# WO(0)'s layernorm in a fused two-layer transformer kernel: four DMA transposes in place of two and two on TensorE, with VectorE held to that layernorm

## The chip, the cores and the metric

One core of one Trainium2 chip runs the whole kernel. The metric is the device time of one execution in microseconds (us). Executions of one kernel agree here within about 0.2% (1238.64 to 1240.82 for the kernel before), so differences of a microsecond in 1240 need several runs and a trace. The "granted clock" is the share of its full clock that TensorE was allowed to run at, as the profile records it.

## The reference, cut to what matters

```python
x = A_x                                        # [1, 2048, 1024], bf16
x = x + attention(layernorm(x), wqkv, wo)      # local, dilated: 8 keys, stride 2, 32 heads of 32
x = x + ffn(layernorm(x), w1, b1, w2, b2)      # gelu, 3584 hidden
x = x + attention(layernorm(x), wqkv, wo)      # the same weights again
x = x + ffn(layernorm(x), w1, b1, w2, b2)
```

The kernel cuts the 2048 positions into four groups of 512. Group n of layer 1 is n = 0..3, of layer 2 n = 4..7. For each n there are the stages QKV(n), attention on VectorE, WO(n) (output projection, residual, layernorm), FFN1(n) and FFN2(n). TensorE needs the normalised tile transposed (features on partitions) to go on.

## The kernel before

All engines are programmed through a framework that orders each engine's instructions itself. The kernel can pin the order of its matmuls (each depends on the one before), and `hold()` on VectorE: no VectorE instruction written after it goes ahead of the last one written before it.

```python
def acc_tile():                                # six PSUM accumulators of 128x512 f32
    return psum.tile([P, T], F32, name="acc", bufs=6)

def ln_tile(t, tt, xnT, on_pe=False, ahead=False):
    mv, rstd = (...) if ahead else ln_stats(t)   # VectorE stats, POOL for 1/sqrt
    xn = ln_norm(t, mv, rstd)                    # VectorE; three buffers named xn
    if on_pe:
        late.append((xn, xnT[:, tt, :, :]))      # transposed later, by TensorE
        return
    sp.dma_start_transpose(xnT[:, tt, :, :], xn[:].rearrange("s (k p) -> s k p", p=P))

def gen_wo(n, pe_from=NTT):
    # ... cut: two weight loads
    for tt in range(NTT):                        # four tiles of 128 positions
        for dh in range(2):                      # a "chunk": 8 matmuls into one accumulator
            # ... cut: the matmuls
            vec.tensor_tensor(out=xs, in0=ps[:], in1=xs, op=ALU.add)
            yield
        ln_tile(t, tt, xnT, tt >= pe_from)

# the schedule around WO(0)
stage(q2, 18)                                    # QKV(2) up to two of eight V chunks
stage(gen_wo(0, 2))                              # tiles 2 and 3 kept for TensorE
stage(q2, sides=each(new_prod, 1, 0, 1, 4, 8) + at(4, transpose_late))   # the other six V chunks
stage(gen_ffn1(0), sides=at(4, attend, 1) + ...) # head sums of group 1 after five FFN1 chunks
# ...
stage(gen_ffn2(0), sides=... + at(23, hold) + at(23, ln_a, 3, None, True))
# then WO(1), QKV(3), ...
```

`new_prod` is VectorE's product of q and k for one slice of the heads, with sums into a tree; `attend` begins with the head sums on TensorE (accumulator `L`), which need the last sum of that tree. FFN2's results leave their accumulators through VectorE (`tmp<-acc`); this is called an eviction below. `x15` is the sixteenth and last tile of 128 positions, `ln_a(3)` the layernorm ahead of QKV(3), and SP the engine whose queue issues the weight loads and the DMA transposes.

## Time and profile before

| | before |
|---|---|
| time, median of the six runs of the comparison | 1239.13 us (1238.64 to 1240.82) |
| span of the profiled run | 1237.2 us |
| TensorE busy | 1231.2 us |
| longest wait of TensorE after the first 100 us | 1.02 us |

The page of the kernel before: busy time by engine, TensorE's granted clock in 40 slices, and the chain of work that ended last.

```profile
span 1237.2 us, 14039 instructions
...
PE 1231.2 (100%) x5841; PEld 632.9 (51%) x5841; DVE 840.0 (68%) x868; ACT 306.3 (25%) x477; POOL 94.3 (8%) x214
...
PEclk9999999999999999999999999999999999999999
...
PE 97%; DVE 1%; POOL 1%; DMA 0%; issue 0%; ACT 0%
```

TensorE (PE) is the bound. A busy PE only says that matmuls were in the pipe, but here 704 of them in a row take 152.05 us in the chain, 216 ns each, so there is hardly a gap. The list of who waited for whom, PE alone, from 100 us to the end:

```profile
PE acc L211 <- DVE xn L93: 1.0, 1, 1.0
```

One wait in 1137 us. Its surroundings in the timeline of the kernel before (columns: start, duration of the merged row, engine, operation, tiles, count, and in brackets the idle time ahead and what ended it):

```profile
139.24 8.80 PE L118 MATMUL acc<-xnT,wt 128*128 128x512 bf16 x40
...
143.57 2.28 DVE L93 TENSOR_TENSOR big<-big 128x4096 bf16<-128x4096 bf16 x1
...
145.89 2.29 DVE L93 TENSOR_TENSOR big<-big 128x4096 bf16<-128x4096 bf16 x1
146.05 2.18 POOL L93 TENSOR_TENSOR rstd<-mv,eps_t 128x1 f32<-128x1 f32 x1 [4.17 <-DVE mv L93]
...
147.87 0.61 PE L211 MATMUL acc<-ident,xn 128*128 128x128 bf16 x8
...
148.89 0.55 DVE L93 TENSOR_SCALAR xn<-x,mv,rstd 128x1024 bf16<-128x1024 bf16 x1 [0.71 <-POOL rstd L93]
...
149.50 0.62 PE L211 MATMUL acc<-ident,xn 128*128 128x128 bf16 x8 [1.02 <-DVE xn L93]
...
149.96 10.53 PE L118 MATMUL acc<-xnT,wt 128*128 128x512 bf16 x48
```

From 147.87 to 149.96 TensorE does 16 transposes and waits for the last tile, 2.09 us in all. The tile is late since VectorE put two sums of 2.2 us ahead of finishing its layernorm, and since POOL's add of one column, 0.2 us elsewhere, took 2.18 us beside the second of them.

### The profile page before, as it was taken

Reading aid. Unit: us, or ns where it says so; the run is one execution under the profiler, and the core shown is the slowest. Engines: PE = TensorE matmul, PEld = TensorE weight load, DVE = VectorE, ACT = ScalarE, POOL = GpSimd, SP = SyncE. Lnnn points to the kernel's source line nnn. Section 1 sums busy time; section 2 is a strip of 40 time slices with the busy share of each in tenths; the row PEclk is TensorE's granted clock in tenths of the full one; section 3 lists DMA queues with packets and bytes.
Section 4 is the critical chain, followed back from the end, with each engine's and each line's share of the span. In section 5 each row is a group of like instructions: output and inputs, shape, how many; then the busy total and the mean of one; then the engine's idle time right before and its main releaser. Section 6 shows DMA issues by size and latency. Waiting matters only on the chain.

```text
span 1237.2 us, 14039 instructions
## 1 busy us (share of the span) xinstructions
PE 1231.2 (100%) x5841; PEld 632.9 (51%) x5841; DVE 840.0 (68%) x868; ACT 306.3 (25%) x477; POOL 94.3 (8%) x214
## 2 busy tenths in 40 slices
PE   9999999999999999999999999999999999999998
PEld 6666544456444564445644455444654444444444
DVE  7989899996985899337994379843597788012001
ACT  4333252023420144101341023510235001300310
POOL 4010210012000100001000010100001002000000
PEclk9999999999999999999999999999999999999999
DMA  9954564576646555656556565566654568556441
GB/s 308 279 179 146 165 198 161 168 176 216 191 156 201 161 177 161 196 168 183 170 157 198 172 182 160 164 198 199 171 170 135 184 200 193 169 157 195 152 136 53
DMA packets 215327, 219.81 MB, mean 178 GB/s; under 512 B 66066, under 2 KB 184992, under 8 KB 212192
## 3 DMA queue, kind: packets, MB, share of 16 engines
q1 hardware_dynamic: 212592, 208.16, 54.7%
q0 software_dynamic: 2672, 10.76, 2.8%
q8 instruction: 45, 0.74, 0.2%
q14 instruction: 18, 0.15, 0.0%
HBM read 197.40 MB, written 6.29 MB: 165 GB/s over the span
## 4 chain that ended last, share of the span: by engine, by line
PE 97%; DVE 1%; POOL 1%; DMA 0%; issue 0%; ACT 0%
PE acc L118 97%; POOL rstd L93 1%; DVE stats L93 1%; PE L L118 0%; DVE x L93 0%; DMA x<-in_A_x_dram 0%; DVE xn L93 0%; DVE big L93 0%; PE acc L211 0%; DVE mv L93 0%; PE L L211 0%; ACT xnT L93 0%
## 5 line engine op out<-in xcount | busy, mean ns | idle before, releaser
L118 PE MATMUL acc<-xnT,wt 128*128 128x512 bf16 (+1 forms) x3376 | 721.7, 376 | 0.6 <-ACT xnT L93 0.6
L118 PEld LDWEIGHTS <-wt 128*128 128x128 bf16 x3376 | 398.6, 119 | 320.9 <-issue 3.9
L118 PE MATMUL acc<-wt,hT 128*128 128x512 bf16 (+1 forms) x1820 | 388.1, 376 | 0.0
L118 PEld LDWEIGHTS <-hT 128*128 128x128 bf16 x1820 | 178.1, 98 | 209.0
L93 DVE TENSOR_TENSOR big<-big 128x1024 bf16<-128x1024 bf16 (+2 forms) x184 | 244.2, 1359 | 1.8
L93 ACT ACTIVATE hT<-acc,b1T 128x512 bf16<-128x512 f32 x224 | 151.8, 687 | 319.8 <-PE acc L118 319.2
L93 DVE TENSOR_TENSOR big<-abc,vT 128x4096 bf16<-128x4096 bf16 x64 | 144.0, 2283 | 49.3 <-DMA abc<-a_d 49.3
L93 DVE TENSOR_TENSOR tmp<-acc,b2bc 128x512 f32<-128x512 f32 x56 | 38.6, 690 | 180.9 <-PE acc L118 177.4
L93 DVE TENSOR_TENSOR big<-qT,kT 128x4096 bf16<-128x4096 bf16 x64 | 143.8, 2285 | 23.7 <-ACT kT L93 23.1
L93 ACT CAST qT<-acc 128x512 bf16<-128x512 f32 x64 | 37.4, 586 | 329.2 <-PE acc L118 329.2
L118 PE MATMUL acc<-wt,oT 128*128 128x512 bf16 x448 | 97.9, 379 | 0.0
L93 DVE BATCH_NORM_STATS2 stats<-x 128x6 f32<-128x512 bf16 x128 | 83.7, 679 | 3.3 <-DMA x<-in_A_x_dram 2.7
L118 PEld LDWEIGHTS <-oT 128*128 128x128 bf16 x448 | 43.8, 98 | 52.9 <-issue 0.2
L93 DVE TENSOR_TENSOR x<-acc,big 128x512 bf16<-128x512 f32 (+1 forms) x9 | 5.7, 633 | 90.0 <-PE acc L118 90.0
L93 ACT CAST vT<-acc 128x512 bf16<-128x512 f32 x64 | 37.5, 586 | 83.7 <-PE acc L118 83.7
L93 POOL TENSOR_TENSOR rstd<-mv,eps_t 128x1 f32<-128x1 f32 x60 | 18.5, 308 | 502.3 <-DVE mv L93 502.3
L93 ACT CAST kT<-acc 128x512 bf16<-128x512 f32 x64 | 37.5, 586 | 71.7 <-PE acc L118 71.7
L93 POOL DMA_DIRECT2D a_d<-a x32 | 19.0, 620 | 410.7 <-DVE a L93 410.7
L93 DVE TENSOR_SCALAR xn<-x,mv,rstd 128x1024 bf16<-128x1024 bf16 x52 | 28.6, 550 | 30.0 <-POOL rstd L93 29.5
L93 DVE TENSOR_TENSOR x<-acc,x 128x512 bf16<-128x512 f32 x64 | 43.0, 672 | 6.1 <-PE acc L118 5.8
L93 DVE TENSOR_TENSOR x<-tmp,x 128x512 bf16<-128x512 f32 x56 | 38.6, 690 | 1.5
L93 POOL TENSOR_TENSOR rstd<-rstd,mhalf 128x1 f32<-128x1 f32 x60 | 33.9, 565 | 4.7
(54 smaller groups left out, 211.3 us busy)
## 6 DMA issues: line engine op xcount, KB each, us to landing
wt<-in_B_w_dram SPq DMA_DIRECT2D x56, 1024.0 KB, 5.5
wt<-in_B_w_dram SPq DMA_DIRECT2D x64, 896.0 KB, 4.7
wt<-in_A_wqkv_dram SPq DMA_DIRECT2D x46, 1024.0 KB, 5.6
wt<-in_A_wo_dram SPq DMA_DIRECT2D x16, 1024.0 KB, 4.9
abc<-a_d POOLq DMA_DIRECT2D x32, 256.0 KB, 4.6
x<-in_A_x_dram SPq DMA_DIRECT2D x16, 256.0 KB, 5.4
out_dram<-x SPq DMA_DIRECT2D x31, 128.0 KB, 1.8
wt<-in_A_wqkv_dram SPq DMA_DIRECT2D x4, 512.0 KB, 6.8
```

Source lines behind the costliest of these rows:

```text
L93: inst = f(*args, **kwargs)
L118: return pe(nc.tensor.matmul(*args, **kwargs))
```

## The change

Its intent: take the 16 transposes and their wait off TensorE. All four tiles of WO(0) go through DMA transposes; VectorE is held so that the products stand behind the layernorm; and the second W1 load is ordered behind the transposes on the SP queue, so that it does not delay them.

```diff
-    def ln_tile(t, tt, xnT, on_pe=False, ahead=False):
+    last_transpose = [None]
+
+    def ln_tile(t, tt, xnT, ahead=False):
         ...
-        if on_pe:
-            late.append((xn, xnT[:, tt, :, :]))
-            return
-        sp.dma_start_transpose(...)
+        last_transpose[0] = sp.dma_start_transpose(...)
@@ gen_ffn1
-            sp.dma_start(wt[:], w1_v[:, :, j4 * 4 * P:(j4 + 1) * 4 * P])
+            load = sp.dma_start(wt[:], w1_v[:, :, j4 * 4 * P:(j4 + 1) * 4 * P])
+            if n == 0 and j4 == 1:
+                dep_order(load, last_transpose[0], "transposes first")
@@ the schedule
-        stage(gen_wo(0, 2))
-        stage(q2, sides=each(new_prod, 1, 0, 1, 4, 8) + at(4, transpose_late))
+        new_prod(1, 4)
+        hold()
+        stage(gen_wo(0))
+        hold()
+        stage(q2, sides=each(new_prod, 1, 0, 1, 5, 8))
```

(Cut: the removal of `late`, `transpose_late` and `pe_from`.)

More of the change, by code (lines that the diff above doesn't have):

```diff
@@ L214, in transpose_on_pe @@
             act.copy(out[:, h * n:(h + 1) * n, :], pst[:, h * n:(h + 1) * n, :])
-    late = []
-    def transpose_late():
-        while late:
-            transpose_on_pe(*late.pop(0))
-    def ln_tile(t, tt, xnT, on_pe=False, ahead=False):
+    last_transpose = [None]
+    def ln_tile(t, tt, xnT, ahead=False):
         mv, rstd = (mv_ahead[:, tt, :], rstd_ahead[:, tt, :]) if ahead else ln_stats(t)
         xn = ln_norm(t, mv, rstd)
-        if on_pe:
-            late.append((xn, xnT[:, tt, :, :]))
-            return
-        sp.dma_start_transpose(xnT[:, tt, :, :], xn[:].rearrange("s (k p) -> s k p", p=P))
+        last_transpose[0] = sp.dma_start_transpose(xnT[:, tt, :, :], xn[:].rearrange("s (k p) -> s k p", p=P))
     first_late = []
@@ L394, in av, with gen_wo @@
         vec.tensor_tensor(out=s["oT"][:, c, :], in0=pv[:, 0, :], in1=pv[:, 1, :], op=ALU.add)
-    def gen_wo(n, pe_from=NTT):
+    def gen_wo(n):
         g = n % NG
@@ L415, in gen_wo @@
                 yield
-            ln_tile(t, tt, xnT, tt >= pe_from)
+            ln_tile(t, tt, xnT)
         del st[n]
```

## The prediction

> **What bounds the kernel.** TensorE. The summary of engines gives PE 1231.2 of 1237.2 us (VectorE 68%), granted clock 1.0; the chain of waits is 97% accumulation matmuls. 704 matmuls take 152.05 us in a long stretch, 216 ns each. The list of PE's waits, after the first 100 us, has one entry: 1.0 us for WO(0)'s last normalised tile. Only what PE need not execute or wait for can be won.
>
> **Removed.** In the timeline, V of QKV(2) pauses at 147.87: eight transposes of tile 2 (0.62), eight of tile 3 that wait 1.02 for VectorE; the next matmul starts at 149.96. These 2.1 us are on the critical path and vanish. The tile was late because of products ahead of the layernorm (2.19 us each) and of POOL's add for rstd, 2.18 us while VectorE worked on large tiles, 0.20 otherwise. The Trainium skill (GPSIMD Engine Reference, 1. Specifications) says POOL shares its SBUF interfaces with VectorE; 2.18 against 0.20 agrees.
>
> **Added at WO(0).** Two more DMA transposes. The last add ends about 140.1; with stats (0.6), aggregate (0.13), POOL (0.9) and normalisation (0.55) the last tile is ready about 142.3; a transpose lands 2.7 us after issue: 145 to 146. FFN1(0) begins at 139.24 + 48 x 0.2157 = 149.6: no wait. The second W1 load leaves about 143.7 instead of 140.5, takes 6.6 to 8.3, is needed at 156.5: no wait. VectorE then owes three products and four sums, 7 x 2.26 = 15.8 us: done about 158.1. PE wants them for the head sums at 158.2: 0 to 0.4 us of wait.
>
> **Moved, 100 us later.** The compiled order also changes where FFN2(0) hands over to WO(1). (a) The SP queue has the third QKV(3) weight load ahead of that group's transposes; before, it came after three. That load waits for FFN2(0)'s last weights, until WO(1) starts (W; 249.03 before). A transpose issued behind such a load landed 1.05 us after it (load 251.01 to 257.2, transpose 258.3), so the first lands at W + 6.3 to 7.4. (b) VectorE has WO(1)'s first adds among FFN2(0)'s four last evictions, and the normalisation of x15, which waits for that first transpose to free its buffer, ahead of the third and fourth. These free the accumulators (ring of six) for WO(1)'s chunks 4 and 5, which PE would start at W + 6.99 and W + 8.74. The third eviction then ends at W + 8.6 to 9.7 (transpose + 2.3 us of VectorE work): stall 1.6 to 2.7 us; the fourth comes 2.45 us later against PE's 1.75: 0.7 more. Before: W + 3.2 and W + 6.1.
>
> **Sum.** 1239.2 - 2.1 + 0.1 + 2.9 = 1240.1 us: a new stall gives the gain back. Range 1236.9 to 1241.8 (low end: no new stall). Faster by over 2%: 0.5%; within 2%: 99%; slower: 0.5%.
>
> **What would show it.** No transposes on PE at 148, FFN1(0) starting at 149.6; POOL's rstd adds 0.2 us in WO(0); head sums at 158.2, waiting under 0.4; WO(1) starting about 247.0; two PE waits on VectorE inside WO(1), about 2.2 and 0.7 us, VectorE idle before x15's normalisation until a transpose lands. Later stages as before.
>
> **What would make it wrong.** If the load doesn't hold the transposes up, x15 is in time and the stall is about 1.4 us (1238.6). If the products come late, head sums wait a microsecond or two more. If the evictions have other accumulators than I count, no stall: 1237.1.

## The result, and the profile after

| | before | after |
|---|---|---|
| median of six runs | 1239.13 us | 1237.67 us (1237.55 to 1237.90) |
| ratio | | 0.9987, 95% interval 0.9974 to 1.0 |
| span of the profiled run | 1237.2 us | 1236.0 us |
| WO(1) starts | 249.03 us | 248.03 us |
| last matmul ends | 1233.99 us | 1232.98 us |

Ratios are the mean time of one kernel's fast runs over the mean of the other's of the same rounds, so not quite the ratio of the medians. The time is inside the predicted range, but on the other side of the time before than the central value of 1240.1: the kernel got about 1.5 us faster, not 0.9 slower. The interval reaches 1.0, so the ratio alone doesn't settle that; but every run of the changed kernel (at most 1237.90) is below every run of before (at least 1238.64), and in the traces TensorE finishes 1.01 us earlier, with that lead already there at WO(1). Another 0.2 us is in the tail behind the last matmul, 3.2 us against 3.0; the remaining 0.3 us is within the spread of the runs (later sets of before have medians 0.03 to 0.35 us lower).

The page after, the same lines:

```profile
span 1236.0 us, 13961 instructions
...
PE 1227.6 (99%) x5775; PEld 632.1 (51%) x5825; DVE 840.5 (68%) x868; ACT 303.8 (25%) x475; POOL 92.3 (7%) x214
...
PEclk9999999999999999999999999999999999999999
...
PE 96%; DVE 2%; DMA 1%; issue 0%; POOL 0%; ACT 0%; SPq 0%
```

The weight loads (PEld) went from 5841 to 5825, the 16 transposes; some 50 matmul records are missing from this trace, so its PE row is not compared. The waits of PE after 100 us:

```profile
PE L L118 <- DVE big L93: 1.1, 1, 1.1
```

The old wait is gone, and another one of the same size is there. The timeline around WO(0) after the change:

```profile
139.19 19.16 PE L118 MATMUL acc<-xnT,wt 128*128 128x512 bf16 x88
139.26 0.55 DVE L93 TENSOR_SCALAR xn<-x,mv,rstd 128x1024 bf16<-128x1024 bf16 x1 [0.38 <-POOL rstd L93]
...
140.32 0.67 DVE L93 TENSOR_TENSOR x<-acc,x 128x512 bf16<-128x512 f32 x1
...
142.04 0.19 POOL L93 TENSOR_TENSOR rstd<-mv,eps_t 128x1 f32<-128x1 f32 x1 [2.83 <-DVE mv L93]
...
142.90 0.55 DVE L93 TENSOR_SCALAR xn<-x,mv,rstd 128x1024 bf16<-128x1024 bf16 x1 [0.93 <-POOL rstd L93]
143.36 2.29 DVE L93 TENSOR_TENSOR big<-qT,kT 128x4096 bf16<-128x4096 bf16 x1
...
154.74 4.62 DVE L93 TENSOR_TENSOR big<-big 128x4096 bf16<-128x4096 bf16 x2
...
159.41 0.62 PE L118 MATMUL L<-big,smat 128*32 128x512 bf16 x8 [1.06 <-DVE big L93]
```

88 matmuls run through where the pause was. FFN1(0) starts without a wait (the last transpose, issued when the tile was ready at about 143.4, landed 2.8 us later, ahead of 149.5). But VectorE now owes three products and four sums after the layernorm, and its last sum ends just ahead of 159.41, 1.06 us after TensorE was ready for the head sums. So the balance on TensorE is -2.09 + 1.06 = -1.03 us, and 1.01 is what the trace shows.

Now the hand-over from FFN2(0) to WO(1), where I had predicted 2.9 us of new stall. First the kernel before, SP's queue and VectorE:

```profile
246.96 3.96 SPq L93 DMA_TRANSPOSE xnT<-xn  x3
...
249.88 0.54 DVE L93 TENSOR_SCALAR xn<-x,mv_ahead,rstd_ahead 128x1024 bf16<-128x1024 bf16 x1
...
251.01 0.88 SPq L93 DMA_DIRECT2D wt<-in_A_wqkv_dram  x1
...
251.57 0.68 DVE L93 TENSOR_TENSOR tmp<-acc,b2bc 128x512 f32<-128x512 f32 x1
...
254.50 0.68 DVE L93 TENSOR_TENSOR tmp<-acc,b2bc 128x512 f32<-128x512 f32 x1
```

The two `tmp<-acc` are the third and fourth eviction of FFN2(0). After the change, SP, VectorE and TensorE:

```profile
236.13 12.45 SPq L93 DMA_DIRECT2D wt<-in_A_wqkv_dram  x3
...
248.03 13.98 PE L118 MATMUL acc<-wt,oT 128*128 128x512 bf16 x63
...
248.64 12.30 SPq L93 DMA_TRANSPOSE xnT<-xn  x5
...
255.62 0.55 DVE L93 TENSOR_SCALAR xn<-x,mv_ahead,rstd_ahead 128x1024 bf16<-128x1024 bf16 x1 [2.04 <-DMA xnT<-xn]
...
257.28 0.67 DVE L93 TENSOR_TENSOR tmp<-acc,b2bc 128x512 f32<-128x512 f32 x1
...
259.60 0.69 DVE L93 TENSOR_TENSOR tmp<-acc,b2bc 128x512 f32<-128x512 f32 x1
```

VectorE did what was predicted: three loads now stand ahead of the transposes, the first transpose lands 6.9 us after its issue instead of 2.8 (W + 7.5, W = 248.03), VectorE idles 2.04 us for it, and the third eviction ends at about W + 9.9 (257.28 + 0.67), the fourth at W + 12.3. Only TensorE does not care: it needed chunk 4's accumulator at about W + 6.9 (four chunks of 1.73 us) and ran its 64 matmuls (63 of them recorded) in 13.98 us, as before. Why not is the first question to the experiments.

### The profile page after: what moved, and what is told of

Same layout as the page of the kernel before. It is cut to its first block, busy times and chain, and to the rows that moved or that the text cites. A ratio compares the mean times of both kernels' runs of the same rounds, so it can differ in the third digit from the quotient of the medians.

```text
span 1236.0 us, 13961 instructions
## 1 busy us (share of the span) xinstructions
PE 1227.6 (99%) x5775; PEld 632.1 (51%) x5825; DVE 840.5 (68%) x868; ACT 303.8 (25%) x475; POOL 92.3 (7%) x214
## 4 chain that ended last, share of the span: by engine, by line
PE 96%; DVE 2%; DMA 1%; issue 0%; POOL 0%; ACT 0%; SPq 0%
PE acc L118 96%; DVE big L93 1%; DVE stats L93 1%; DMA x<-in_A_x_dram 1%; PE L L118 0%; POOL rstd L93 0%; DVE x L93 0%; DVE xn L93 0%; SPq L93 0%; DVE mv L93 0%; ACT xnT L93 0%; PE L L211 0%; ACT kT L93 0%; ACT vT L93 0%; POOL zhalo L93 0%
## 5 line engine op out<-in xcount | busy, mean ns | idle before, releaser
L93 POOL TENSOR_TENSOR rstd<-mv,eps_t 128x1 f32<-128x1 f32 x60 | 14.5, 241 | 500.9 <-DVE mv L93 500.8
```

Of the source, the lines that this page charges most:

```text
L93: inst = f(*args, **kwargs)
```

## The experiments

Ten kernels ran, all correct, all with five timed rounds. They ran in three calls, each on another chip and with its own runs of the kernel before: medians 1239.10 (the four from ring_after to ring_turn_first), 1238.78 (hold_only, no_hold, no_dep and sums_later) and 1238.82 (no_hold_fill and hold_only_later). Most of the intervals contain 1, so differences of about 1 us rest on the traces and on sets of runs that do not overlap. "PE end" is the end of the last matmul in the one profiled run; the matmuls behind WO(0) start between 139.13 and 139.42 us in the twelve traces, so 0.3 us between two PE ends is not read as a difference.

| run | median (us) | ratio to before, 95% interval | PE end (us) | waits of PE after 100 us (us) |
|---|---|---|---|---|
| before | 1239.13 | 1 | 1233.99 | 1.0 last tile |
| the change | 1237.67 | 0.9987 (0.9974 to 1.0) | 1232.98 | 1.1 head sums |
| ring_after | 1242.19 | 1.0027 (1.0015 to 1.004) | 1237.47 | 3.0 accumulator, 1.1 head sums |
| ring_before | 1238.92 | 1.0 (0.9988 to 1.0013) | 1234.07 | 1.0 last tile |
| turn_first | 1237.76 | 0.999 (0.9977 to 1.0004) | 1233.01 | 1.1 head sums |
| ring_turn_first | 1238.49 | 0.9996 (0.9984 to 1.0009) | 1233.77 | 1.1 head sums, 0.4 accumulator |
| hold_only | 1237.84 | 0.9991 (0.9979 to 1.0004) | 1232.92 | none |
| no_hold | 1241.26 | 1.0016 (1.0003 to 1.0028) | 1236.72 | 2.8 transpose |
| no_dep | 1237.87 | 0.9991 (0.9978 to 1.0003) | 1232.99 | 1.1 head sums |
| sums_later | 1236.62 | 0.998 (0.9967 to 0.9994) | 1231.94 | none |
| no_hold_fill | 1239.44 | 1.0005 (0.9992 to 1.0019) | 1234.95 | none (gap filled) |
| hold_only_later | 1237.90 | 0.9993 (0.998 to 1.0006) | 1232.98 | none |

### Which accumulator a chunk gets: ring_after and ring_before

My stall rested on "ring of six": the seventh user of the accumulators gets the first one's. The compiled program of the changed kernel says otherwise. This is its list of WO(1)'s chunks with the PSUM bank (the piece of accumulator memory) and the VectorE instruction that each waits for (no view of the profile shows it):

```
chunk 2  bank 4  after FFN2(0)'s 1st eviction
chunk 3  bank 1  after chunk 0's own residual add
chunk 4  bank 5  after chunk 1's own residual add
chunk 5  bank 3  after FFN2(0)'s 2nd eviction
chunk 6  bank 2  after FFN2(0)'s 3rd eviction
chunk 7  bank 4  after chunk 2's own residual add
```

Banks are handed on in the order in which VectorE's instructions release them. To see whether this and nothing else is where the stall went, the accumulators got six names used in turn:

```diff
+    acc_n = [0]
+    def acc_ring(shape, dtype):
+        acc_n[0] += 1
+        return psum.tile(shape, dtype, name=f"acc{(acc_n[0] - 1) % 6}_", bufs=1)
     def acc_tile():
-        return psum.tile([P, T], F32, name="acc", bufs=6)
+        return acc_ring([P, T], F32)
```

(and likewise at the two other users of that pool). In the compiled programs TensorE, VectorE and GpSimd have the same order of instructions as in the kernel it was made from. ring_before has it on every engine; in ring_after two weight loads change places with transposes on SP, behind the five transposes of this hand-over, and two instructions move on ScalarE. The wait below names the third eviction, so these moves don't explain it.

> The changed kernel with its six accumulators forced into a strict ring (the assumption of the prediction); the order of instructions on every engine is the same as in the changed kernel, only the accumulator banks differ. If the failed step of the prediction was only the ring: VectorE's third and fourth evictions of FFN2(0) end where they do now (about W + 9.8 and W + 12.2, W = start of WO(1)), and PE waits for them, about 2.9 us before WO(1)'s chunk 4 and 0.6 before chunk 5; time about 1241.2 us. Rival: the late evictions never matter to PE (something else takes them up): no new wait, 1237.7.

> Control: the kernel before with the same strict ring. Its evictions end at W + 3.2 and W + 6.1, ahead of need, so no new wait and 1239.1 us (within 0.4). If the ring itself costs something, this is slower as well and ring_after must be read against it.

The control did not move (1238.92 us). With the changed kernel's order the ring costs 4.5 us: 1242.19, where turn_first below, which times like the change, took 1237.76. TensorE and VectorE in ring_after (accumulators now have numbers, and lines are counted six further on):

```profile
253.28 1.89 PE L124 MATMUL acc__2168<-wt,oT 128*128 128x512 bf16 x7
...
257.41 0.67 DVE L99 TENSOR_TENSOR tmp<-acc__1965,b2bc 128x512 f32<-128x512 f32 x1
...
258.14 3.18 PE L124 MATMUL acc__2189<-wt,oT 128*128 128x512 bf16 x8 [2.97 <-DVE tmp L99]
261.15 1.89 PE L124 MATMUL acc__2199<-wt,oT 128*128 128x512 bf16 x8
```

`acc__2189` is chunk 4, and it waits 2.97 us for the third eviction, as the prediction's sum had it (2.9 expected). So the arithmetic of the stall was right and its premise wrong: the rival, that late evictions never matter, falls. Expected 1241.2, found 1242.2: after the wait chunk 4's eight matmuls take 3.01 us instead of 1.73, at half the granted clock, which is taken up again under no_hold; the second wait (0.6 expected) is then hidden.

### Whether the load ahead of the transposes is what made VectorE late: turn_first and ring_turn_first

```diff
+            if after is not None:
+                dep_order(load, after, "transposes first")     # in load_qkv
-        wk = load_qkv(1)
+        wk = load_qkv(1, last_ln_a[0] if n == 3 else None)     # ln_a(3)'s last transpose
```

> The changed kernel with the third QKV(3) weight load held behind ln_a(3)'s four transposes on the SP queue. Theory: VectorE's idle 2.0 us before x15's normalisation vanishes (the load held the transpose up), and the time stays 1237.7 (within 0.3), since PE did not wait there. Rival (the late VectorE costs something hidden): 1 us or more faster.

> Both: strict ring and the load held behind the transposes. Theory: the third eviction ends at about W + 6.7, in time for chunk 4, the fourth at about W + 9.3, 0.5 us late for chunk 5; time about 1238.2, so that 3 of ring_after's 3.5 us come from the load standing ahead of the transposes. Rival (the stall of ring_after has another cause, the order of VectorE alone): about 1240 to 1241.

VectorE in turn_first, and TensorE's one wait in WO(1) in ring_turn_first:

```profile
251.18 0.54 DVE L93 TENSOR_SCALAR xn<-x,mv_ahead,rstd_ahead 128x1024 bf16<-128x1024 bf16 x1
...
257.44 1.89 PE L124 MATMUL acc__2199<-wt,oT 128*128 128x512 bf16 x8 [0.38 <-DVE tmp L99]
```

In turn_first the normalisation of x15 has no wait for a transpose any more (it starts at 251.18, and the list of waits of VectorE there has no DMA), and the time is that of the change, 1237.76. In ring_turn_first the ring costs 0.7 us (1238.49 against the 1237.76 of turn_first) instead of 4.5, with one wait of 0.4. Both as expected. The compiled order of VectorE moves a little with this edit too, so the two runs price the load and the order that follows from it together; but the idle time named the transpose. That VectorE is 2 us late at this place is thus real, and costs nothing as long as the banks are handed on as they are. The margin is not large: chunk 6 waits for the third eviction, over at about 257.9, and starts at about 258.4 (248.03 + 6 x 1.73).

### Which half of the change brings the gain: hold_only, no_hold, no_dep

hold_only is the kernel before with the two holds and `new_prod(1, 4)` in front; tiles 2 and 3 stay on TensorE. no_hold is the changed kernel without them:

```diff
-        new_prod(1, 4)
-        hold()
         stage(gen_wo(0))
-        hold()
-        stage(q2, sides=each(new_prod, 1, 0, 1, 5, 8))
+        stage(q2, sides=each(new_prod, 1, 0, 1, 4, 8))
```

no_dep only drops the two lines that order the second W1 load.

> The kernel before with only the second half of the change: VectorE held to WO(0)'s adds and layernorm, tiles 2 and 3 still transposed on PE. Theory: the last tile is normalised at about 143.4, so the pause in V shrinks from 2.1 us to about 1.0 (16 transposes, no wait); head sums then come at 159.2, level with the products, wait 0 to 0.3: 1237.8 to 1238.3 us, nearly all of the gain without any DMA transpose. Rival (the gain comes from taking the transposes off PE): about 1239.

> The changed kernel without the two holds: four DMA transposes, VectorE free to put products first as before. Theory: the last tile is again normalised at about 149.4, its transpose lands at about 152.2, FFN1(0) would start at 149.6: PE waits about 2.6 us there, none at the head sums; about 1239.7 us, no better than before or 0.5 worse. Rival (DMA transposes alone give the gain): 1237.7 or less.

> The changed kernel without the ordering of the second W1 load behind the transposes: the load then stands between the second and third transpose. Theory: the last two transposes land about a microsecond after that load, near 148, still ahead of 149.6: no wait for them, 1237.7 (within 0.3); this part of the change is idle. Rival: the transposes come late and PE waits 0.5 to 2 us at FFN1(0)'s start.

TensorE in hold_only:

```profile
147.77 1.06 PE L211 MATMUL acc<-ident,xn 128*128 128x128 bf16 x16
148.66 10.57 PE L118 MATMUL acc<-xnT,wt 128*128 128x512 bf16 x48
159.34 0.61 PE L118 MATMUL L<-big,smat 128*32 128x512 bf16 x8
```

The 16 transposes take 0.89 us without a wait, and TensorE then comes to the head sums at 159.34 and does not wait for the products. PE end is 1232.92, that of the full change (1232.98). By PE end the holds alone bring all of the gain, and by the medians too: 1237.84 us against 1237.87 for no_dep, the change without its load order. The rival, that it comes from taking transposes off TensorE, falls. With the DMA transposes TensorE is 1.0 us earlier at the head sums (158.35), and waits 1.06 there.

no_hold shows the reverse. The last tile is again normalised at 149.0, its transpose lands 2.8 us after TensorE wanted it, and the kernel is slower than before: 1241.26. A wait of 2.6 us had been expected, and with it 1239.7 us. What came on top is in the stretches after the wait, in no_hold (columns: stretch, its length, then busy time of PE, PEld, DVE, ACT and POOL with counts, granted clock, DMA share, GB/s):

```profile
152.70:154.70 2.00, 1.96 (x7) 0.82 (x8) 1.97 (x2) 0.67 (x1) 0.00 (x0) 0.69 0.89 291
154.70:156.70 2.00, 2.00 (x6) 0.62 (x5) 1.97 (x2) 1.30 (x2) 0.00 (x0) 0.50 1.09 384
156.70:158.70 2.00, 2.00 (x10) 0.93 (x9) 2.00 (x2) 0.62 (x1) 0.00 (x0) 0.96 1.09 387
```

The granted clock is at half for 3.41 us, from 153.46 to 156.87 (found with narrower stretches), which begins 0.7 us after the wait is over. In ring_after such a spell of 3.41 us (257.37 to 260.78) begins 0.8 us before the wait ends, 2.20 us after TensorE had gone idle at 255.17, so a part of it cost nothing. The inner part of both spells, same columns, no_hold and then ring_after:

```profile
153.50:156.80 3.30, 3.30 (x10) 1.11 (x8) 3.23 (x3) 1.97 (x2) 0.00 (x0) 0.50 1.08 381
...
257.50:260.60 3.10, 2.46 (x6) 0.86 (x6) 3.10 (x7) 0.00 (x0) 0.74 (x2) 0.50 0.57 126
```

The 40 matmuls behind the wait take 10.41 us (152.74 to 163.15) instead of 8.63 (40 at the 216 ns of full speed), 1.78 more. Of the five runs four have a mean clock of 0.998 or 0.999 and took 1241.07 to 1241.47; one has 1.0 and took 1239.49, near the 1239.7 expected. (In ring_after, too, one run of five has 1.0.)

no_dep is as fast as the change (1237.87): the load then goes out at 138.53, between the second and the third transpose, and nothing waits for it. That part of the change is idle here.

### Whether idleness lowers the clock: no_hold_fill

The DMA engines are nearly full just where the slow matmuls are, so the clock could have been a companion and not the cause. Into the gap go 12 matmuls whose result nobody reads:

```diff
+    fill(12)        # 12 matmuls of the identity, 512 columns each
     stage(gen_ffn1(0), sides=...)
```

> The kernel without the holds, whose PE wait of 2.84 us ahead of FFN1(0) was followed by matmuls at half the granted clock, with 12 matmuls on the identity (2.6 us, result unused) put into that gap so that PE is not idle. Theory (the idle stretch lowers the clock, and that is the 1.5 us more than I expected): clock 1.0 in the trace after the gap, head sums 10.4 - 8.6 = 1.8 us earlier, 1239.5 us in all runs. Rival (the slow matmuls come from the crowded DMA at that moment, or from something else than PE's idleness): still about 1241.3.

The same stretches in no_hold_fill, same columns:

```profile
152.70:154.70 2.00, 2.00 (x10) 0.92 (x11) 1.97 (x2) 0.62 (x1) 0.00 (x0) 1.00 0.89 270
154.70:156.70 2.00, 2.00 (x11) 0.88 (x9) 1.97 (x2) 1.75 (x3) 0.00 (x0) 1.00 1.09 385
156.70:158.70 2.00, 2.00 (x11) 0.89 (x10) 2.00 (x2) 0.96 (x2) 0.00 (x0) 1.00 1.08 386
```

The same DMA load, but clock 1.00, head sums at 161.37 instead of 163.15 (1.78 us earlier), and 1239.22 to 1239.78 us in all five runs: useless work in the gap makes the kernel 1.8 us faster. The edit also changed VectorE's order, at WO(1) above all, and moved a few instructions on ScalarE and SP; TensorE has no other wait after 100 us in either kernel. The Trainium skill (TensorE: Matmul & The Clock Gate, Why this matters for your kernels) asks for no idle gaps over about 3 us; here waits of 2.84 and 2.97 us were enough, and in the second the clock fell 2.20 us after TensorE had gone idle, while the waits of 1.0 to 1.1 us left the clock at 1.00.

### Taking the new wait away: sums_later and hold_only_later

```diff
-    stage(gen_ffn1(0), sides=at(4, attend, 1) + at(4, spread, 1) + at(4, hold) + ...
+    stage(gen_ffn1(0), sides=at(5, attend, 1) + at(5, spread, 1) + at(5, hold) + ...
```

> The changed kernel with the head sums of group 1 (and the softmax and spread behind them) one FFN1(0) chunk later. Theory: the 1.06 us wait of PE for the last product sum (159.3 against 158.35) is the whole of what the change gave back, so it vanishes: about 1236.6 us and no PE wait after the first 100 us. Rival: VectorE is then late elsewhere (softmax, spread, av) and the wait turns up again: 1237.5 or more.

> VectorE held, tiles 2 and 3 transposed on PE, and the head sums one chunk later. There was no wait at the head sums in the run with the holds alone, so moving them gains nothing: 1237.8 us (within 0.3). Against the changed kernel with later head sums (1236.6) this prices what the DMA transposes bring once the head sums are out of the way: about 1.2 us. Rival (later head sums gain by themselves): 1237.2 or less.

sums_later is the best version found: 1236.62 us, ratio 0.998 (0.9967 to 0.9994), faster than both kernels. TensorE in it, with no wait from 100 us to the end:

```profile
144.67 15.49 PE L118 MATMUL acc<-xnT,wt 128*128 128x512 bf16 x71
160.09 0.62 PE L118 MATMUL L<-big,smat 128*32 128x512 bf16 x8
```

Its PE end is 1231.94, that is 2.05 us ahead of before: the whole of the 2.09 us pause. The later softmax made TensorE wait nowhere else. In hold_only_later the move gains nothing (1237.90, PE end 1232.98). So the two parts of the original change combine like this, in PE end relative to before: holds alone -1.07, DMA transposes added -1.01, head sums one chunk later as well -2.05. The DMA transposes are worth 1.0 us, but only once their lead is not spent waiting for the products.

## Why the prediction was right or wrong

The range held the time and "within 2%" was right. The central value was 2.4 us too high (1240.1 against 1237.67), and it had the sign of the difference wrong. That the range held is no support for the mechanism: it was wide enough for the stall and for no stall, and of the two terms that were off (2.9 us of stall too much, about 1 us at the head sums too little) one hid a part of the other, which is luck. Term by term:

- **Removed, 2.1 us: right.** TensorE runs through where it paused, and sums_later, with no other wait, ends 2.05 us ahead of before.
- **POOL's add at 0.2 us in WO(0): right.** 0.18 to 0.19 us for all four tiles. The Trainium skill (GPSIMD Engine Reference, 1. Specifications) states that POOL's SBUF interfaces are shared with VectorE; 2.18 us beside a large VectorE sum and 0.19 without one agree with it.
- **No wait at FFN1(0) for the transposes or for W1: right.** no_dep shows besides that the ordering of the load was not needed.
- **Head sums, "0 to 0.4 us of wait": too small, 1.06 us.** The mis-sized step is "the last tile is ready about 142.3": it was 143.4. I had the last residual add end about 140.1, as soon as TensorE delivered. But VectorE ran its list in order: it idled 0.38 us for POOL ahead of the third tile's normalisation, and that and a stats instruction stood ahead of the last add, which began at 140.32 and ended at 140.99, 0.9 us later than assumed. The way from there to the normalised tile took 2.5 us instead of 2.2; the wait for POOL in it was 0.93 us, as counted. The seven products and sums then took 15.9 us (15.8 had been counted).
- **The stall in WO(1), 2.9 us: not there. This is the step that failed**, and in it the words "These free the accumulators (ring of six) for WO(1)'s chunks 4 and 5". The load ahead of the transposes, the late transpose, VectorE's idle time and the times of the evictions came about as predicted (the transpose at W + 7.5 and the third eviction at W + 9.9, 0.1 and 0.2 past my brackets). But chunks 4 and 5 had other banks, released earlier. Forced into a ring, the same instructions do wait 2.97 us. The prediction had named this as its third way to be wrong, with 1237.1 us; with the head sums at their measured 1.06 that case gives 1239.2 - 2.1 + 1.1 = 1238.2, against 1237.67 measured.

The bank of every accumulator stood in the compiled program of the changed kernel, which I had: it was not looked up. That was the avoidable mistake.

Two things stay open. The trace explains 1.0 of the 1.5 us between the medians, and 0.2 in the tail; the rest I put down to the spread of the runs, without a test. And what length of wait lowers the clock was not measured: 1.1 us did not, 2.20 us had in the trace of ring_after, and a wait of 2.84 us did in four runs of five and not in the fifth.

## What to carry to other kernels

Work taken off the bounding engine only counts until that engine meets its next dependency: after moving work, look for the next consumer (here the head sums) and move it by the same amount; that turned 1.0 us into 2.05. Holding a busy engine to the critical piece brought the gain of the change here, not moving the piece to another unit. Before predicting a stall on a recycled buffer, read from the compiled program which buffer is meant, for pools need not go round in a ring; and when TensorE would idle for 2 to 3 us, count a possible spell of slower clock as well as the wait (here 3.41 us at half, so up to 1.7 us).

## What the Trainium skill lacked or had wrong

- TensorE: Matmul & The Clock Gate. Part 1 gives an idle window of about 3.4 us before the clock halves, and Why this matters for your kernels gaps over about 3 us. Here waits of 2.84 and 2.97 us, both shorter than that window, each came with one spell of 3.41 us at a granted clock of 0.50 (with each kernel the mean clock of the run was lowered in four runs of five); it began 0.7 us after the first wait and 0.8 us before the end of the second, and cost 1.78 and 1.28 us. That one run in five escaped, and that the spells lie differently to the waits, fits the page's statement that the window runs freely; it was not tested.
- DMA: Bandwidth & Descriptors has no figure for a transpose queued behind a plain load: alone it landed 2.7 to 2.8 us after issue, right behind a 1 MB load of 6.3 us on the same queue 6.9 us after. Its section Queues, rings and completion order says that descriptors of a ring are consumed in order, and this agrees.
- No page says how recycled PSUM accumulators are assigned by the framework: with six of them, WO(1)'s chunk 4 took the bank of chunk 1 and not the one that was next in turn.
